# A linear-attention block with a gated feed-forward on one core: a new written order, ten transposes by DMA, constants set elsewhere, and the last unit's feed-forward in parts

## The chip, the core and the metric

The kernel runs on one core of one Trainium2 chip. The time is device microseconds of one execution, and the median over several runs counts. A profiled execution gives its own time and a trace of every instruction and DMA on the engines PE (matmul), DVE (vector), ACT (scalar), POOL (GpSimd) and SP (which only issues DMAs here).

## What is computed

Shapes: batch 4, 8 heads, 768 steps, head size 48, float32. The attention is a recurrence over time with a decay `w` for every key channel; its output, 3072 rows of 384, goes through a feed-forward layer of width 1024 with a softmax-scaled activation, a normalization and a gain.

```python
for t in range(S):
    cur = einsum('bhd,bhe->bhde', u * k[t], v[t])
    y[t] = einsum('bhd,bhde->bhe', r[t], state + cur)
    state = w[t][..., None] * state + einsum('bhd,bhe->bhde', k[t], v[t])
x = y as [B*S, H*D]
h = x @ w_in
solu = h * softmax(h)
ln = (solu - mean) / sqrt(var + 1e-6) * g_ln
out = ln @ w_out
```

## The kernel before, in words

Time is cut into six chunks of 128 steps, and with four batches this makes 24 units; unit `i` is chunk `i // 4` of batch `i % 4`. A unit goes through some thirty stages, each a short function. What stage of which unit runs when is not found by loops: the string ORDER (line 21) lists all of it, about 900 words, and the last loop (line 522) calls one function for each. A word is a stage, the unit's number and, after a dot, the engine (`a` ACT, `d` DVE, `p` POOL), the issuing queue (`s` SP, `a` ACT) or the PSUM bank (`s0` to `s3` one bank, `b0` and `b1` two banks). `InOrder` (line 75) keeps each engine's instructions in the written order; an engine waits where its next instruction's operands are not there. So what stands between two words on one engine is what that engine does in between.

The stages, by their words:
- Loads: LW, LK, LR, LV fetch w, k, r, v of a unit, 192 KB each, in pieces of 192 bytes, into rings of NIO = 7 buffers. LI0 to LI2 (512 KB each) fetch w_in, LO0 and LO1 (768 KB each) w_out, LG and LU the gain and u.
- Attention: lw is the logarithm of the decays (ACT), cum sums them over time (PE), ex takes the exponential (ACT), kp scales k and r with it (DVE), krk and krr transpose the scaled k and r by PE (four each), kr copies them to SBUF. M makes the scores (PE), m copies them and masks them (on DVE, or on ACT with the mask sel on POOL). p, q, dg, dv make the term with u (POOL and DVE); vb rounds v. S, et, st carry the state to the next chunk. Y makes the attention output (PE), y copies it to SBUF.
- Feed-forward: X transposes y by PE (three), xT copies it, H makes h for all 1024 columns (24 matmuls of 128 columns), e is its exponential (ACT), he their product (DVE), hq its square. Oa and Ob multiply by w_out, four of eight column blocks each; for each block there is a matmul of 385 columns (384 outputs and the sum) and two of one column (softmax sum and square sum), all into one PSUM bank. sq, qm, lv (two ACT instructions: lv and rs) make the scale, o applies it, out stores 192 KB from SP.
- Once: wi rounds w_in to bf16; gw multiplies w_out by the gain, mn and mc take its column mean, ce subtracts it; Oa of unit 0 needs all of these. us and uc spread u over the partitions. hot only keeps PE busy.

The constants (masks, identity, block patterns) are set by DVE and POOL ahead of the first word. Two stages are defined and not called: `turned_kr` (line 444), which transposes a unit's scaled k and r from SBUF to SBUF by one DMA on SP, and `turned_x` (line 447), which does so for y.

Of the kernel before, what the change touches and what calls it, by code (L numbers as in the profile page):

```python
# [8 lines left out]
F32 = mybir.dt.float32  # L9
BF16 = mybir.dt.bfloat16  # L10
# [11 lines left out]
LW0.a LK0.s LU0.a LR0.s LW1.a LW2.s hot4.s3 LG0.s LK1.s lw0 LV0.a cum0.b0 LR1.s us0.s0 ex0 hot2.s3 uc0 lw1 LV1.s  # L22
p0 kp0 LW3.a LK2.a LR2.s krk0.s3 q0 krr0 cum1.b1 kr0.a hot2.s2 LV2.s LK3.a M0.b0 LR3.s p1 gs0.s1 ex1 m0.d
hot3.s3 LI1.s lw2 q1 dg0 cum2.b0 lw3 hot2.s3 kp1 vb0.p LI0.a S0.s2 dv0 vb1.a dg1 hot1.s3 ex2 Y0.is0 et0 LV3.a
cum3.b1 LI2.s p2 kp2 krk1.s3 gc0 LO0.s ex3 st0 LW4.s krk2.s1 q2 krr1 LO1.s krr2 kp3 kr1.a hot3.s2 dv1 LK4.s
kr2.d y0.a p3 M1.b0 LK5.a S1.s2 dg2 krk3.s3 vb2.a m1.d krr3 et1 wi0.a S2.s0 wi1.p M2.b1 st1 X0.s1 kr3.a m2.d
Y1.is2 LR4.s wi2.p et2 y1.a M3.b0 xT0.d LV4.a X1.s3 q3 m3.d H0.b1 dv2 gw1.a dg3 gw2.d e0 Y2.is2 LW5.s xT1.d
gw3.p st2 H1.b0 y2.a he0 lw4 gw0.a X2.s1 LR5.s e1 gw7.d cum4.b1 gw4.d hot2.s3 gw6.d gw5.d ex4 he1 vb3.p mn0.s3
LW6.s LV5.a dv3 xT2.a LK6.s kp4 S3.s0 mc0 Y3.is2 LR6.s lw5 ce6.d krk4.s1 ce3.d hq0.a cum5.b0 ce4.d krr4 ce2.d
H2.b1 ce7.d ex5 LW7.s ce1.d ce5.d ce0.d y3.a LK7.s p4 kp5 et3 Oa0.s3 lw6 e2 LR7.s kr4.d p5 krk5.s2 cum6.b0 st3  # L30
hq1.a Ob0 vb4.p he2 LW8.s q4 krr5 ex6 S4.s1 LK8.s kr5.d sq0 M4.b1 lw7 Oa1.s0 kp6 et4 m4.a LR8.s X3.s2 qm0 st4
vb5.p M5.b0 xT3.a cum7.b1 dg4 sel4 lv0 krk6.s1 LV6.s Ob1 m5.d ex7 LW9.s dv4 lw8 S5.s2 kp7 o0.a krr6 LK9.s p6
cum8.b0 sq1 et5 Y4.ns3 kr6.d ex8 H3.b1 q5 LV7.s y4.d hq2.a kp8 q6 LR9.s krk7.s1 e3 X4.s3 st5 LW10.s vb6.p M6.b0
krr7 xT4.d Oa2.s2 dg5 m6.a LK10.s qm1 kr7.d dv5 krk8.s3 lv1 Ob2 he3 out0 sel6 o1.a lw9 M7.b0 out1 dg6 S6.s1 sq2
m7.a LV8.s hq3.d krr8 cum9.b1 LR10.s Y5.ns0 vb7.p qm2 kr8.d lv2 H4.b0 p7 LW11.s et6 y5.d ex9 st6 p8 lw10 kp9
LV9.s X5.s3 S7.s0 e4 Oa3.s1 q7 o2.d vb8.a he4 out2 cum10.b1 dv6 xT5.a krk9.s2 et7 LK11.s ex10 Y6.ns3 q8 krr9 st7
LV10.s H5.b0 hq4.a kp10 sel7 LR11.s kr9.a y6.d M8.b1 dg7 LW12.s S8.s0 lw11 m8.d Ob3 dv7 et8 e5 LV11.s vb9.p
krk10.s3 st8 X6.s2 LK12.s p9 M9.b1 he5 xT6.a Y7.ns0 sq3 m9.a krr10 LR12.s S9.s2 dg8 cum11.b0 et9 LW13.s y7.d
H6.b1 lw12 dv8 ex11 kr10.d LK13.s p10 qm3 lv3 kp11 Oa4.s0 LR13.s e6 q9 st9 X7.s3 cum12.b0 LW14.s xT7.a Ob4 he6
p11 ex12 LV12.s krk11.s2 sel9 sq4 Y8.ns3 o3.a kp12 H7.b1 hq5.a out3 vb10.p qm4 y8.d q10 LK14.s lv4 dg9 M10.b0 e7  # L40
Oa5.s1 LR14.s m10.d vb11.p q11 o4.a krr11 LW15.s X8.s3 lw13 dg10 Ob5 p12 xT8.a out4 he7 kr11.a S10.s0 dv9 S11.s3
LV13.s dg11 sq5 hq6.a Y9.ns2 vb12.p qm5 cum13.b0 y9.d dv10 LK15.s H8.b1 et10 ex13 st10 LR15.s et11 lw14 kp13
Oa6.s2 LW16.s e8 hq7.d krk12.s0 lw15 M11.b0 p13 st11 LK16.s Ob6 lv5 he8 o5.a q12 krr12 m11.a Y10.ns3 out5 kr12.d
krk13.s1 cum14.b1 LR16.s y10.d sq6 krr13 sel11 ex14 cum15.b0 LW17.s kr13.d Oa7.s0 ex15 qm6 LV14.s kp14 p14
Y11.ns3 lw16 X9.s1 Ob7 kp15 lv6 dv11 LK17.s vb13.a xT9.d p15 o6.a M12.b1 y11.d M13.b0 m12.a X10.s1 out6 m13.d
krk14.s2 q13 S12.s3 LR17.s hq8.a krr14 H9.b1 dg12 LV15.s vb14.p xT10.d sq7 q14 et12 qm7 st12 LW18.s lv7 krk15.s1
dg13 e9 X11.s3 sel12 H10.b0 o7.d kr14.a out7 he9 dv12 LK18.s Y12.ns0 xT11.a p16 krr15 LR18.s Oa8.s2 e10 y12.d
kr15.d q15 LV16.s cum16.b1 he10 S13.s0 ex16 dv13 Ob8 LV17.s et13 kp16 q16 X12.s3 LW19.s Y13.ns1 sq8 xT12.a st13
M14.b0 vb15.p M15.b1 LK19.s m14.a y13.d krk16.s3 S14.s0 hq9.d krr16 LR19.s m15.a S15.s1 p17 qm8 kr16.d H11.b0
LW20.s et14 dg14 lv8 sel14 st14 et15 LK20.s dg15 H12.b1 e11 vb16.p o8.d sel15 st15 out8 lw17 Oa9.s3 he11 LV18.s  # L50
e12 vb17.p dv14 S16.s0 LV19.s hq10.a he12 Ob9 dv15 LR20.s et16 cum17.b0 st16 q17 Y14.ns2 LV20.s ex17 X13.s1
y14.d M16.b1 sq9 Oa10.s0 lw18 kp17 LW21.s m16.a Y15.ns2 qm9 xT13.d LK21.s cum18.b0 hq11.d lv9 krk17.s1 lw19
H13.b1 LR21.s o9.d p18 vb18.a dg16 ex18 LV21.s y15.d dv16 krr17 e13 Ob10 kp18 LW22.s sel16 X14.s3 hq12.a kr17.d
S17.s2 LK22.s cum19.b0 q18 he13 Oa11.s1 xT14.a LR22.s ex19 p19 X15.s3 lw20 M17.b1 out9 xT15.d Ob11 sq10 kp19
vb20.p m17.a LW23.s q19 Y16.ns3 qm10 dg17 et17 vb19.a cum20.b0 p20 LV22.s y16.d lv10 H14.b1 dg18 sq11 ex20 sel17
LK23.s st17 lw21 o10.d LR23.s Oa12.s3 e14 kp20 dv17 krk18.s2 Ob12 out10 hq13.a p21 qm11 he14 krk19.s0 LV23.s
lv11 krr18 q20 cum21.b0 sq12 o11.d krr19 ex21 H15.b1 p22 qm12 kr18.d out11 lv12 kr19.d vb21.p Oa13.s1 dv18 kp21
e15 X16.s2 o12.d Y17.ns0 xT16.a M18.b0 hq14.a y17.d out12 krk20.s3 Ob13 he15 lw22 X17.s0 m18.a krk21.s2 xT17.d
krr20 cum22.b1 dg19 krr21 sq13 sel18 ex22 qm13 S18.s0 dg20 H16.b0 kr20.d hq15.a q21 kr21.d lv13 kp22 Oa14.s3
dv19 e16 dv20 M19.b1 et18 Y18.ns2 he16 m19.a Ob14 lw23 sel19 y18.d M20.b1 sq14 M21.b0 o13.d Oa15.s2 m21.a st18  # L60
out13 m20.d krk22.s1 X18.s0 cum23.b0 xT18.a krr22 Ob15 ex23 hq16.d vb22.p dg21 kr22.a Y19.ns0 q22 kp23 H17.b1
vb23.a dv21 qm14 sq15 y19.d lv14 Y20.ns1 e17 p23 o14.d H18.b0 dg22 out14 sel21 qm15 y20.d lv15 krk23.s0 he17 e18
Oa16.s3 dv22 krr23 o15.a he18 q23 Ob16 kr23.a out15 X19.s1 M22.b1 xT19.d M23.b0 hq17.d X20.s2 S19.s0 xT20.a
hq18.d Oa17.s1 m22.a dg23 Y21.ns2 et19 m23.a sel22 st19 H19.b1 sq16 sel23 qm16 y21.d lv16 Oa18.s0 e19 dv23
X21.s2 Ob17 he19 H20.b0 sq17 o16.d xT21.d out16 Y22.ns3 qm17 e20 Y23.ns2 y22.d Ob18 y23.d hq19.a he20 H21.b1
lv17 o17.d X22.s3 Oa19.s2 e21 out17 xT22.d hq20.d X23.s1 sq18 H22.b0 he21 xT23.d Ob19 qm18 hq21.d e22 H23.b1
sq19 lv18 qm19 he22 Oa20.s3 e23 o18.d hq22.d Oa21.s1 out18 lv19 he23 Ob20 o19.d Ob21 sq20 hq23.d out19 Oa22.s0
sq21 qm20 qm21 lv20 Oa23.s2 lv21 o20.d o21.d out20 Ob22 out21 Ob23 sq22 qm22 lv22 sq23 qm23 o22.d lv23 out22
o23.a out23
# [27 lines left out]
def kernel(  # L97
# [14 lines left out]
    C = 128  # L112
# [20 lines left out]
    def bank(shape, dtype, slot, name):  # L133
# [15 lines left out]
    dve.memset(warm, 0.0)  # L149
    uti_neg = consts.tile([C, C], BF16)  # L150
    pool.memset(uti_neg, -1.0)
    pool.affine_select(out=uti_neg, in_=uti_neg, compare_op=ALU.is_ge, fill=0.0, base=0,
                       pattern=[[1, C]], channel_multiplier=-1)
    uts = consts.tile([C, C], BF16)
    pool.memset(uts, 1.0)
    pool.affine_select(out=uts, in_=uts, compare_op=ALU.is_gt, fill=0.0, base=0,
                       pattern=[[1, C]], channel_multiplier=-1)
    ident_f = consts.tile([C, C], F32)
    pool.memset(ident_f, 0.0)
    pool.affine_select(out=ident_f, in_=ident_f, compare_op=ALU.not_equal, fill=1.0, base=0,  # L160
                       pattern=[[-1, C]], channel_multiplier=1)
    ident = consts.tile([C, C], BF16)
    pool.tensor_copy(out=ident, in_=ident_f)

    halves = consts.tile([C, C], BF16)
    pool.memset(halves, 0.0)
    pool.memset(halves[0:2, :], 1.0)
    pool.affine_select(out=halves[0:2, :], in_=halves[0:2, :], compare_op=ALU.is_ge, fill=0.0, base=0,
                       pattern=[[1, C]], channel_multiplier=-64)
    pool.affine_select(out=halves[0:2, :], in_=halves[0:2, :], compare_op=ALU.is_gt, fill=0.0, base=64,  # L170
                       pattern=[[-1, C]], channel_multiplier=64)
    off_blocks = consts.tile([C, HP, 2], BF16)
    pool.memset(off_blocks, 0.0)
    pool.memset(off_blocks[0:2], -30000.0)
    pool.affine_select(out=off_blocks[0:2], in_=off_blocks[0:2], compare_op=ALU.not_equal, fill=0.0, base=0,
                       pattern=[[0, HP], [-1, 2]], channel_multiplier=1)

    one_col = consts.tile([C, 2], BF16)
    dve.memset(one_col, 1.0)
    inv_col = consts.tile([C, 1], BF16)  # L180
    dve.memset(inv_col, 1.0 / RDF)
    ones_row = consts.tile([1, C], F32)
    dve.memset(ones_row, 1.0)

    lw_t = ring("lw", NLW, [C, H, 64], BF16)
    kp_t = ring("kp", NKP, [C, 2, H, 64], BF16)
# [369 lines left out]
```

The softmax here doesn't subtract the row's maximum and nothing guards it: scores larger than these inputs give would overflow.

## Time and profile before

| | |
|---|---|
| Median of 3 runs | 152.28 us (151.85 to 153.1) |
| Profiled execution, its own time | 153.27 us |
| Its span, first to last instruction | 151.6 us |
| Busy: PE, weight load | 137.2 us (91%), 106.6 us (70%) |
| Busy: DVE, ACT, POOL | 127.9 us (84%), 117.9 us (78%), 94.9 us (63%) |
| Moved by DMA | 27.08 MB, 179 GB/s on the mean |

Busy time is the sum over the whole span, and the span has stages that are limited by different things. Two more views are needed: the page's 40 slices of 3.8 us, in which a digit is the busy share in tenths, and the chain of waits, which follows the end back to what released it. Nearly all instructions carry line 89, that of the recorder, so groups are told apart by the tile that they write: `o_ps` is Oa and Ob, `h_ps` is H, `kr_ps` is krk and krr, `x_ps` is X. Matmuls overlap in the pipeline: the mean of one (325 ns for o_ps, 219 ns for h_ps) is longer than its share of PE's time.

### The profile page before, as it was taken

The numbers are of one execution on the slowest core, as the hardware profiler recorded it, in microseconds if no ns is written. First come the engines' busy times: TensorE is split into PE (matmuls) and PEld (weight loads), VectorE is DVE, ScalarE is ACT, GpSimd is POOL, SyncE is SP. The second block draws the span as 40 slices with busy tenths as digits, with TensorE's granted clock in tenths as the row PEclk, the third lists the DMA queues.
The fourth block names the chain that finished last, engine by engine and source line by source line (L and its number), as shares of the span: only waits on it lengthen the run. The fifth ranks groups of instructions, "written<-read, shape, count | busy, mean of one in ns | idle before, by whom it ended". The sixth has DMA issues, their size and how long they took to land.

```text
span 151.6 us, 5258 instructions
## 1 busy us (share of the span) xinstructions
PE 137.2 (91%) x2156; PEld 106.6 (70%) x2158; DVE 127.9 (84%) x235; ACT 117.9 (78%) x238; POOL 94.9 (63%) x127
## 2 busy tenths in 40 slices
PE   4799787879999997999988999999999999999980
PEld 1145566467788776888777797878887888889650
DVE  5209797999999996999976999999998998688940
ACT  3465766599999997999798688999898997484442
POOL 7484993531879859993849999299847682500000
PEclk9999999999999999999999999999999999999997
DMA  5999999999983999989699999898950111011142
GB/s 110 259 257 334 405 335 255 178 210 188 224 179 121 229 217 193 215 176 241 142 243 208 230 175 232 162 230 193 248 164 6 52 56 52 4 52 56 52 160 104
DMA packets 104825, 27.08 MB, mean 179 GB/s; under 512 B 100313, under 2 KB 104418, under 8 KB 104802
## 3 DMA queue, kind: packets, MB, share of 16 engines
q1 hardware_dynamic: 94256, 24.26, 69.6%
q10 hardware_dynamic: 10546, 2.49, 7.3%
q8 instruction: 17, 0.28, 0.7%
q14 instruction: 6, 0.05, 0.1%
HBM read 22.03 MB, written 4.72 MB: 176 GB/s over the span
## 4 chain that ended last, share of the span: by engine, by line
PE 54%; DMA 12%; SPq 10%; DVE 8%; ACT 6%; POOL 4%; issue 4%; ACTq 0%; POOLq 0%
PE o_ps L89 22%; PE h_ps L89 13%; SPq L89 10%; DMA w_in<-in_w_dram 6%; PE kr_ps L89 4%; PE y_ps L89 4%; DMA kr_in<-in_r_dram 4%; PE s_ps L89 3%; PE cum_ps L89 3%; PE m_ps L89 3%; DMA v_in<-in_v_dram 3%; PE x_ps L89 2%; DVE he L89 1%; POOL m L89 1%; DVE w L89 1%
## 5 line engine op out<-in xcount | busy, mean ns | idle before, releaser
L89 PE MATMUL o_ps<-w,he 128*128 128x385 bf16 x192 | 45.7, 325 | 0.1
L89 PE MATMUL h_ps<-xT,win_sb 128*128 128x128 bf16 x576 | 35.9, 219 | 0.3 <-DVE xT L89 0.3
L89 PEld LDWEIGHTS <-win_sb 128*128 128x128 bf16 x576 | 33.0, 98 | 0.9 <-issue 0.4
L89 PE MATMUL o_ps<-inv_col,e 128*128 128x1 bf16 x192 | 31.7, 165 | 0.0
L89 DVE TENSOR_TENSOR he<-h_ps,e 128x1024 bf16<-128x1024 f32 x24 | 29.1, 1216 | 2.7 <-ACT e L89 2.5
L89 PE MATMUL o_ps<-one_col,hq 128*128 128x1 bf16 x192 | 31.3, 163 | 0.0
L89 ACT ACTIVATE e<-h_ps 128x1024 bf16<-128x1024 f32 x24 | 24.5, 1020 | 4.7 <-PE h_ps L89 4.6
L89 DVE TENSOR_TENSOR kp<-cum_ps,kr_in 128x768 bf16<-128x768 f32 x24 | 22.7, 948 | 5.9 <-ACT cum_ps L89 5.6
L89 PEld LDWEIGHTS <-hq 128*128 128x128 bf16 x192 | 18.5, 96 | 12.8
L89 POOL TENSOR_TENSOR p<-kr_in 128x384 bf16<-128x384 f32 x24 | 24.4, 1018 | 3.7 <-DMA kr_in<-in_r_dram 3.6
L89 POOL TENSOR_TENSOR dv<-vb,dg 128x384 bf16<-128x384 bf16 x24 | 19.8, 830 | 9.6 <-DVE dg L89 7.4
L89 POOL TENSOR_SCALAR_AFFINE_SELECT m<-m 128x1024 bf16<-128x1024 bf16 x15 | 16.8, 1120 | 13.4 <-ACT sq L89 5.8
L89 POOL TENSOR_TENSOR q<-p,u_bc 128x384 bf16<-128x384 bf16 x24 | 21.8, 911 | 1.9 <-ACT u_bc L89 1.7
L89 PEld LDWEIGHTS <-kp 128*128 128x128 bf16 x272 | 17.4, 98 | 6.0 <-DVE kp L89 2.1
L89 ACT ACTIVATE cum_ps<-cum_ps 128x768 f32<-128x768 f32 x24 | 19.2, 802 | 3.0 <-PE cum_ps L89 2.9
L89 PE MATMUL kr_ps<-ident,kp 128*128 128x128 bf16 x192 | 18.0, 222 | 2.3 <-ACT gr L89 0.8
L89 PEld LDWEIGHTS <-he 128*128 128x128 bf16 x192 | 18.4, 96 | 0.9
L89 PEld LDWEIGHTS <-e 128*128 128x128 bf16 x192 | 18.4, 96 | 0.5 <-issue 0.2
L89 ACT ACTIVATE lw<-w_in 128x384 bf16<-128x384 f32 x24 | 12.4, 523 | 4.1 <-DMA w_in<-in_w_dram 4.1
L89 ACT CAST m<-m_ps 128x1024 bf16<-128x1024 f32 x15 | 15.0, 1013 | 0.7 <-PE m_ps L89 0.6
L89 DVE TENSOR_TENSOR m<-m_ps,keep 128x1024 bf16<-128x1024 f32 x9 | 10.9, 1215 | 4.2 <-PE m_ps L89 4.2
L89 ACT ACTIVATE hq<-he 128x1024 bf16<-128x1024 bf16 x13 | 13.7, 1057 | 0.0
(82 smaller groups left out, 262.5 us busy)
## 6 DMA issues: line engine op xcount, KB each, us to landing
kr_in<-in_r_dram SPq DMA_DIRECT2D x24, 192.0 KB, 4.3
out_dram<-o SPq DMA_DIRECT2D x24, 192.0 KB, 3.2
kr_in<-in_k_dram SPq DMA_DIRECT2D x21, 192.0 KB, 3.5
w_in<-in_w_dram SPq DMA_DIRECT2D x21, 192.0 KB, 4.2
v_in<-in_v_dram SPq DMA_DIRECT2D x20, 192.0 KB, 4.1
wout_f<-in_moe_w_out_dram SPq DMA_DIRECT2D x2, 768.0 KB, 7.7
win_f<-in_moe_w_in_dram SPq DMA_DIRECT2D x2, 512.0 KB, 5.1
v_in<-in_v_dram ACTq DMA_DIRECT2D x4, 192.0 KB, 4.2
```

Source lines behind the costliest of these rows:

```text
L89: made = make(*args, **kwargs)
```

## The change

- ORDER is written anew. The first loads come in another order and on other queues: LW0 to LW2 and R0, R1 ahead of K0, and all of units 0 to 4 and W5 stand ahead of the second half of w_out. Engines of some copies change.
- For units 19 to 23 krk, krr, kr and X, xT are gone; KD and XD, the two stages on SP that were not called, take their place.
- The constants move into a stage `pc`: the memsets to DVE, four selects stay on POOL; `halves` and `off_blocks` use partitions 0 and 32 and need no select; `keep` and `uts` are one tile. u and the row of ones are bf16 for the u matmul.
- Fifteen stores and LG are issued from POOL.
- Unit 23: H is made in two halves (Ha, Hb), e, he, hq likewise; the three sums go to a PSUM bank of their own (Sa, Sb), the left and right 192 output columns to a bank each (Mal, Mbl and Mar, Mbr), with two scalings and two stores.

```diff
 ORDER = """
-LW0.a LK0.s LU0.a LR0.s LW1.a LW2.s hot4.s3 LG0.s LK1.s lw0 LV0.a cum0.b0 LR1.s us0.s0 ex0 hot2.s3 uc0 lw1 LV1.s
-p0 kp0 LW3.a LK2.a LR2.s krk0.s3 q0 krr0 cum1.b1 kr0.a hot2.s2 LV2.s LK3.a M0.b0 LR3.s p1 gs0.s1 ex1 m0.d
-hot3.s3 LI1.s lw2 q1 dg0 cum2.b0 lw3 hot2.s3 kp1 vb0.p LI0.a S0.s2 dv0 vb1.a dg1 hot1.s3 ex2 Y0.is0 et0 LV3.a
-cum3.b1 LI2.s p2 kp2 krk1.s3 gc0 LO0.s ex3 st0 LW4.s krk2.s1 q2 krr1 LO1.s krr2 kp3 kr1.a hot3.s2 dv1 LK4.s
-kr2.d y0.a p3 M1.b0 LK5.a S1.s2 dg2 krk3.s3 vb2.a m1.d krr3 et1 wi0.a S2.s0 wi1.p M2.b1 st1 X0.s1 kr3.a m2.d
...
-hq18.d Oa17.s1 m22.a dg23 Y21.ns2 et19 m23.a sel22 st19 H19.b1 sq16 sel23 qm16 y21.d lv16 Oa18.s0 e19 dv23
-X21.s2 Ob17 he19 H20.b0 sq17 o16.d xT21.d out16 Y22.ns3 qm17 e20 Y23.ns2 y22.d Ob18 y23.d hq19.a he20 H21.b1
-lv17 o17.d X22.s3 Oa19.s2 e21 out17 xT22.d hq20.d X23.s1 sq18 H22.b0 he21 xT23.d Ob19 qm18 hq21.d e22 H23.b1
-sq19 lv18 qm19 he22 Oa20.s3 e23 o18.d hq22.d Oa21.s1 out18 lv19 he23 Ob20 o19.d Ob21 sq20 hq23.d out19 Oa22.s0
-sq21 qm20 qm21 lv20 Oa23.s2 lv21 o20.d o21.d out20 Ob22 out21 Ob23 sq22 qm22 lv22 sq23 qm23 o22.d lv23 out22
-o23.a out23
+LG0.p pc0 LW0.s LR0.a LU0.s LW1.a hot6.s3 LW2.a LR1.s lw0 ur0 LK2.s LK0.a cum0.b0 LW3.s us0.s0 LK1.a hot4.s3 ex0
+LR2.s LV0.a lw1 lw2 LK3.s cum1.b1 uc0 hot4.s3 kp0 p0 ex1 LW4.a kp1 krk0.s3 q0 gs0.s2 LR3.a cum2.b0 krr0 ex2
+hot2.s1 vb0.p kr0.d LV1.s p1 S0.s1 LK4.a dg0 krk1.s0 LR4.s lw3 M0.b1 hot5.s3 q1 m0.d LI0.s dv0 lw4 dg1 cum3.b1
+et0 p2 hot3.s3 kp2 LV2.a ex3 cum4.b0 q2 LI1.a krr1 kp3 krk2.s3 ex4 LO0.s p3 krr2 kr1.d gc0 vb1.a LW5.s krk3.s2
+st0 LI2.a krr3 dg2 p4 LV4.s M1.b1 LV3.a S1.s0 kp4 kr2.a hot3.s1 m1.d wi0.p LO1.s et1 kr3.a M2.b0 krk4.s1 LK5.s
...
+xT14.d H13.b0 o9.d ex19 out9 lw21 kp19 krk18.s2 e13 Oa11.s3 dg17 KD19 hq12.d krr18 xT15.a H14.b1 lv10 he13
+kr18.a LK22.s LR22.s Y16.ns0 o10.d e14 cum20.b0 LW23.s y16.d S16.s2 dg18 vb17.a Oa12.s1 out10 et16 he14 hq13.a
+dv17 X16.s0 Ob11 sel17 ex20 st16 cum21.b1 xT16.d sq11 Ob12 kp20 p20 ex21 S17.s2 hq14.a KD20 kp21 vb18.p M18.b0
+q19 Y17.ns0 lw22 qm11 m18.d H15.b1 et17 q20 sq12 KD21 lv11 o11.a qm12 y17.d p21 lv12 M19.b0 st17 LK23.s S18.s3
+lw23 m19.d p22 Oa13.s0 LR23.s e15 out11 dv18 X17.s2 et18 dg19 LV21.s o12.a M20.b0 he15 Ob13 xT17.a q21 m20.a
+Y18.ns1 vb19.p st18 out12 cum22.b1 H16.b0 dg20 ex22 p23 y18.d sq13 qm13 kp22 lv13 Oa14.s2 vb20.p e16 dv19 o13.d
+KD22 M21.b1 q22 X18.s3 m21.a S19.s1 he16 Ob14 vb21.p LV22.s hq15.a out13.p dg21 LV23.s cum23.b1 dg22 H17.b0 dv20
+et19 sq14 ex23 qm14 dv21 xT18.a kp23 Y19.ns0 hq16.a sel20 Oa15.s3 st19 KD23 lv14 y19.d H18.b1 q23 o14.a vb22.a
+XD19 sel21 e17 Oa16.s1 dv22 e18 Ob15 he17 out14.p Y20.ns0 he18 Ob16 hq17.a M22.b0 sq15 y20.d M23.b1 Y21.ns2
+m22.d m23.a XD20 Oa17.s0 hq18.a y21.d sel23 H19.b1 dg23 XD21 sq16 vb23.a qm15 lv15 dv23 Y22.ns2 e19 H20.b0 y22.d
+o15.d XD22 qm16 he19 Oa18.s2 out15.p e20 Ob17 he20 H21.b1 sq17 lv16 hq19.d qm17 o16.d Y23.ns3 lv17 Ob18 hq20.a
+y23.d out16 o17.d XD23 Oa19.s1 sq18 e21 qm18 out17.p Oa20.s3 lv18 H22.b0 o18.d he21 out18.p Ob19 e22 hq21.d
+Ha23.b1 sq19 qm19 he22 lv19 Oa21.s0 ea23 Ob20 hea23 Ob21 sq20 o19.a qm20 hq22.d hqa23.a Hb23 out19.p lv20
+Oa22.s2 sq21 eb23 qm21 o20.a heb23 Sa23.s1 lv21 Ob22 out20.p hqb23.d o21.d Sb23 sq22 Mal23.s3 qm22 out21.p sq23
+lv22 Mar23.s0 qm23 Mbl23 lv23 o22.d Mbr23 ol23.a out22.p or23.d outl23 outr23.a
 """
...
-    pool.memset(uti_neg, -1.0)
-    pool.affine_select(out=uti_neg, in_=uti_neg, compare_op=ALU.is_ge, fill=0.0, base=0,
-                       pattern=[[1, C]], channel_multiplier=-1)
...
-    pool.tensor_copy(out=ident, in_=ident_f)
...
+    ident_f = consts.tile([KF, KF], F32)
+    ones_row = consts.tile([1, C], BF16)
+    keep = uts
+
+    def constants(i, x):
+        dve.memset(warm, 0.0)
+        dve.memset(uti_neg, -1.0)
+        dve.memset(uts, 1.0)
+        dve.memset(ident, 0.0)
+        dve.memset(ident_f, 0.0)
+        pool.affine_select(out=uti_neg, in_=uti_neg, compare_op=ALU.is_ge, fill=0.0, base=0,
+                           pattern=[[1, C]], channel_multiplier=-1)
+        pool.affine_select(out=uts, in_=uts, compare_op=ALU.is_gt, fill=0.0, base=0,
+                           pattern=[[1, C]], channel_multiplier=-1)
+        pool.affine_select(out=ident, in_=ident, compare_op=ALU.not_equal, fill=1.0, base=0,
+                           pattern=[[-1, C]], channel_multiplier=1)
+        pool.affine_select(out=ident_f, in_=ident_f, compare_op=ALU.not_equal, fill=1.0, base=0,
+                           pattern=[[-1, KF]], channel_multiplier=1)
+        dve.memset(one_col, 1.0)
+        dve.memset(inv_col, 1.0 / RDF)
+        dve.memset(ones_row, 1.0)
+
+        dve.memset(halves, 0.0)
+        dve.memset(off_blocks, 0.0)
+        for row, own in ((0, 0), (32, 1)):
+            dve.memset(halves[row:row + 1, 64 * own:64 * own + 64], 1.0)
+            dve.memset(off_blocks[row:row + 1, :, 1 - own], -30000.0)
+        for j in range(max(NLW, NKP)):
+            if j < NLW:
+                dve.memset(lw_t[j][:, :, D:], 0.0)
+            if j < NKP:
+                dve.memset(kp_t[j][:, :, :, D:], 0.0)
+        dve.memset(mean_w, -1.0 / DF)
+        dve.memset(w2[:, :, DM:], 1.0 / RDF)
...
+    u_b = consts.tile([1, DM], BF16)
...
-    queue = {"s": sp, "a": act}
+    queue = {"s": sp, "a": act, "p": pool}
...
+    def round_u(i, x):
+        dve.tensor_copy(out=u_b, in_=u_row)
...
-        pe.matmul(ps["u"], lhsT=ones_row, rhs=u_row, start=True, stop=True)
+        pe.matmul(ps["u"], lhsT=ones_row, rhs=u_b, start=True, stop=True)
...
-    def hidden(i, x):
-        xT = xT_t[i % NWK]
-        h_ps = live[i]["h_ps"] = bank([128, KF, C], F32, x, "h_ps")
-        for f in range(KF):
+    def hidden_part(i, f0, f1):
+        xT, h_ps = xT_t[i % NWK], live[i]["h_ps"]
+        for f in range(f0, f1):
             for j in range(KM):
                 pe.matmul(h_ps[:, f, :], lhsT=win_sb[:, j, f * 128:(f + 1) * 128], rhs=xT[:, j, :],
                           start=(j == 0), stop=(j == KM - 1))
 
-    def hidden_exp(i, x):
-        act.activation(out=e_t[i % NWK], in_=live[i]["h_ps"], func=EXP)
-
-    def hidden_mul(i, x):
-        dve.tensor_mul(out=he_t[i % NWK], in0=live[i]["h_ps"], in1=e_t[i % NWK])
-
-    def hidden_square(i, x):
-        he, hq = he_t[i % NWK], hq_t[i % NWK]
+    def hidden(i, x):
+        live[i]["h_ps"] = bank([128, KF, C], F32, x, "h_ps")
+        hidden_part(i, 0, KF)
+
+    def hidden_a(i, x):
+        live[i]["h_ps"] = bank([128, KF, C], F32, x, "h_ps")
+        hidden_part(i, 0, KF // 2)
+
+    def hidden_b(i, x):
+        hidden_part(i, KF // 2, KF)
+
+    ALL, LOW, HIGH = slice(0, KF), slice(0, KF // 2), slice(KF // 2, KF)
+
+    def hidden_exp(i, x, part=ALL):
+        act.activation(out=e_t[i % NWK][:, part], in_=live[i]["h_ps"][:, part], func=EXP)
+
+    def hidden_mul(i, x, part=ALL):
+        dve.tensor_mul(out=he_t[i % NWK][:, part], in0=live[i]["h_ps"][:, part], in1=e_t[i % NWK][:, part])
+
+    def hidden_square(i, x, part=ALL):
+        he, hq = he_t[i % NWK][:, part], hq_t[i % NWK][:, part]
         if x == "a":
             act.activation(out=hq, in_=he, func=SQUARE)
         else:
...
                       skip_group_check=True)
 
     def output_a(i, x):
-        live[i]["o_ps"] = bank([C, DM + 3], F32, x, "o_ps")
+        L = live[i]
+        L["o_ps"] = bank([C, DM + 3], F32, x, "o_ps")
+        L["o"], L["sums"] = L["o_ps"][:, :DM], L["o_ps"][:, DM:]
         output(i, 0)
 
     def output_b(i, x):
         output(i, 1)
 
+
+    HALF = {"l": slice(0, DM // 2), "r": slice(DM // 2, DM)}
+
+    def columns_of(i, x, side, part):
+        if part == 0:
+            live[i]["o" + side] = bank([C, DM // 2], F32, x, "o_ps")
+        for f in range(part * KF // 2, (part + 1) * KF // 2):
+            pe.matmul(live[i]["o" + side], lhsT=he_t[i % NWK][:, f, :], rhs=w2[:, f, HALF[side]],
+                      start=(f == 0), stop=(f == KF - 1))
+
+    def sums_of(i, x, part):
+        if part == 0:
+            live[i]["sums"] = bank([C, 3], F32, x, "o_ps")
+        to = live[i]["sums"]
+        for f in range(part * KF // 2, (part + 1) * KF // 2):
+            pe.matmul(to[:, 0:1], lhsT=he_t[i % NWK][:, f, :], rhs=w2[:, f, DM:], start=(f == 0), stop=False,
+                      skip_group_check=True)
+            pe.matmul(to[:, 1:2], lhsT=e_t[i % NWK][:, f, :], rhs=inv_col, start=False, stop=False,
+                      skip_group_check=True)
+            pe.matmul(to[:, 2:3], lhsT=hq_t[i % NWK][:, f, :], rhs=one_col[:, :1], start=False, stop=(f == KF - 1),
+                      skip_group_check=True)
+
     def sums(i, x):
-        act.activation(out=sq_t[i % NWK], in_=live[i]["o_ps"][:, DM:DM + 2], func=SQUARE)
+        act.activation(out=sq_t[i % NWK], in_=live[i]["sums"][:, 0:2], func=SQUARE)
 
...
-    def scaled_out(i, x):
-        o_ps, rs, o = live[i]["o_ps"], rs_t[i % NWK], o_t[i % NWK]
+    def scaled_out(i, x, side=""):
+        rs, o = rs_t[i % NWK], o_t[i % NWK][:, HALF.get(side, slice(0, DM))]
         if x == "d":
-            dve.tensor_scalar(out=o, in0=o_ps[:, :DM], scalar1=rs, scalar2=None, op0=MULT)
+            dve.tensor_scalar(out=o, in0=live[i]["o" + side], scalar1=rs, scalar2=None, op0=MULT)
         else:
-            act.activation(out=o, in_=o_ps[:, :DM], func=COPY, scale=rs)
-
-    def store(i, x):
+            act.activation(out=o, in_=live[i]["o" + side], func=COPY, scale=rs)
+
+    def store(i, x, side=""):
         c, b = units[i]
-        sp.dma_start(out=out[b * S + c * C:b * S + (c + 1) * C, :], in_=o_t[i % NWK])
+        cols = HALF.get(side, slice(0, DM))
+        queue[x or "s"].dma_start(out=out[b * S + c * C:b * S + (c + 1) * C, cols], in_=o_t[i % NWK][:, cols])
+
+    def of_part(stage, *part):
+        return lambda i, x: stage(i, x, *part)
 
     stages = dict(
+        pc=constants,
...
+        Ha=hidden_a, Hb=hidden_b,
+        **{name + tag: of_part(stage, part) for name, stage in dict(e=hidden_exp, he=hidden_mul, hq=hidden_square).items()
+           for tag, part in (("a", LOW), ("b", HIGH))},
+        **{name + side: of_part(stage, side) for name, stage in dict(o=scaled_out, out=store).items() for side in "lr"},
+        **{name + tag + side: of_part(columns_of, side, part) for name in "M" for tag, part in (("a", 0), ("b", 1))
+           for side in "lr"},
+        Sa=of_part(sums_of, 0), Sb=of_part(sums_of, 1),
```

## The prediction

> **What bounds the kernel now.** I read the page's slices first, then its chain of waits, then busy time by stretches, then the landings of the early loads, then the waits.
>
> ```profile
> PE   4799787879999997999988999999999999999980
> DMA  5999999999983999989699999898950111011142
> 34.00:146.40 112.40, 109.94 (x1882) 90.41 (x1880) 103.83 (x176) 95.21 (x196) 73.16 (x86) 1.00 0.71 156
> 92.00:146.00 54.00, 53.94 (x915) 44.43 (x914) 49.78 (x88) 42.97 (x90) 27.91 (x33) 1.00 0.45 109
> ```
>
> A slice is 3.8 us. DMA is full from the second slice to the 29th (110 us) and nearly empty after; PE has gaps in the first nine slices and none that shows after. In the stretch rows the columns are the length, then PE, weight load, DVE, ACT and POOL busy, clock, DMA share, GB/s. So there are three stages: loads set the pace up to about 34 us, PE from there to 146.4 us (DVE close behind with 103.8 of 112.4), and a tail that is pure latency. In the second stage a microsecond taken from PE's own work is worth a microsecond, if nothing new is waited for. What a stage costs PE stands in the chain, as one piece for one stage:
>
> ```profile
> 105.84 0.47 PE kr_ps L89 x8
> 121.96 1.34 PE h_ps L89 x24
> 129.49 0.83 PE o_ps L89 x12
> 135.65 0.17 PE x_ps L89 x3
> 140.38 5.98 PE o_ps L89 x84
> 146.38 0.18 ACT sq L89
> 148.20 0.58 ACT o L89
> ```
>
> Columns: start, length, engine and tile, instructions. I use such spacings and not the page's durations, since matmuls overlap (219 ns each, but 24 of them in 1.34 us): krk with krr 0.46, X 0.18, H 1.34, Oa or Ob 0.83, M 0.33, S 0.47, Y 0.38, cum 0.33. All words of the order summed this way, without warm-ups, make 123 us of PE. At 33.73 us, where the first Oa starts, 108.0 of it is left; PE ends at 146.36, so this stage holds 146.36 - 33.73 - 108.0 = 4.6 us of scattered waits. The start is read from these waits:
>
> ```profile
> POOL vb L89 <- DMA v_in<-in_v_dram: 6.1, 4, 2.8
> ACT lw L89 <- DMA w_in<-in_w_dram: 4.1, 3, 2.2
> POOL p L89 <- DMA kr_in<-in_r_dram: 3.6, 3, 2.0
> DVE w L89 <- ACT mean_sb L89: 0.4, 1, 0.4
> ```
>
> (Total us, times, longest.) From the completion events in the trace: a 192 KB load lands every 0.83 us early on, the weights (3 MB) come at about 400 GB/s, LI2 lands at 18.54, LO1 at 24.96; from there gains, column mean and centring on DVE take until 33.67, and Oa0 starts.
>
> [...] loads of both queues land interleaved at one rate. [...] in this trace TensorE does eight in 0.47 us, since they are pipelined; no DMA transpose occurs in it. [...] no DMA is issued from POOL before.
>
> **The change part by part.**
>
> **Transposes of units 19 to 23.** Removed from PE: 5 x 0.46 (k, r) + 5 x 0.18 (y) = 3.2 us, all in the PE-bound stage: whole gain. Gone too are ten PSUM copies (0.35 to 1.02 us each) on DVE and ACT; with the reassignments DVE falls by 6 us in sum and ACT rises by 2.5. Nothing on those is booked: PE hides them. Added: ten DMA transposes on SP, where loads 22 and 23 and four stores stand behind them. What covers them is PE work between producer and consumer: from KD19, 20, 21, 22, 23 to the M of that unit 8.3, 3.9, 5.9, 8.9 and 4.6 us; from Y19 to Y23 to the H of that unit 7.3, 4.8, 6.0, 7.6 and 5.1, of which some 1.2 us go to the y copy and its turn on DVE. A small DMA out of SBUF here takes 1.82 us at the least from issue to landing (the stores near 132 us). [...] I take 4 and 3 us: about 1 us of wait in all, at M20 and H20. No gain beyond the 3.2 is possible from it.
>
> **The start.** Before LO1's landing 17 unit loads have to land in the old order, 21 in the new (five full units and W5), and two of the three w_in parts wait on ACT's queue behind its compute. Four more loads x 0.83 = 3.3 us: LO1 at 28.2. By the same count LI2 comes at about 24 instead of 18.5. K0 is issued behind lw0 on ACT, so kp0 (6.55 before) comes at about 9; PE is idle then, so I book nothing. From LO1 on, ACT does gw0, gw3, gw6, xT3, ex5, e2, mc0 and DVE he2 and seven centrings; with the rows' durations Oa0 starts at 37.3 against 33.73. But PE has by then done more: 18.9 us of useful work precede Oa0 in the new order, against 15.1. What is left is 101.3. So the later start and the larger share done before cancel, within 1.5 us either way, and what stays is the 3 us less PE work: 37.3 + 101.3 + 4.6 = 143.2 for PE's end, against 146.4. I keep the 4.6 us of scattered waits: DVE is lighter, but new waits on POOL stand against it.
>
> **Constants and u.** POOL's row of constants ran from 0.80 to 4.83; now DVE does the memsets (about 1 us more before kp0, which waits for DMA anyway), and POOL four selects of 0.29 us after the issue of LG. cum0 started at 4.89, waiting for lw0 until W0 had landed at 4.29: cover of 2 us. u in bf16 shortens the u matmul from 1.64 us at a time when PE idles. Ten more warm-up matmuls (0.21 each) fill the same idle time. All zero; without that cover at most 1 us.
>
> **Stores on POOL.** Fifteen stores leave SP. [...] POOL has 73 us of work in 112, so it has room, but it is in order: out7 waits for o7 ahead of dv and vb work. Zero, to +1.5.
>
> **The tail.** Before, after PE's end at 146.36: sq, qm, lv, rs for two units, o, issue at 148.80, landing at 150.65, end at 151.6: 5.2 us. After, the sums of unit 23 are complete before its 16 column matmuls (about 0.08 each, 1.3 us by half of 0.165), which covers the 0.9 us of sq, qm, lv, rs. After PE's end there remain half an o (about 0.4), issue and landing 1.85, and the end 0.95: 3.3 to 3.5. Gain 1.7. PE pays 0.25 for the extra columns, which the 101.3 holds already. The halves of e and he let PE wait less for H23, where Ob20 and Oa21 cover it anyway.
>
> **Sum.** -3.2 (PE's end) - 1.7 (tail) + 1.0 (transposes) = -3.9: span 147.7 against 151.6. The profiled execution itself took 153.27, 1.0 over the median of 152.28 shown; carried to the median, 148.4.
>
> **The rivals.** (1) *Slower: the DMA transposes outlast their cover.* Place: M20 and M21, H20 and Ha23, where PE is in order and everything behind waits. Price: with 8 us for k, r and 6 for y, about 3 + 2 at the two M and 2.4 + 0.5 + 1.5 at the H, some 9 us: 152.28 - 4.9 + 9 = 156. [...] It decides from where waits exceed 4.9 us: about 6 us for k, r and 5 for y. For it: KD20, KD21 are issued back to back behind three loads at one queue; 128-row transposes by DMA are nowhere in the trace. Against: DMA is nearly idle after 110 us, and the stores land in 1.8. (2) *The start costs what the rest brings.* If the weights behind ACT's compute come 3 us later than counted, Oa0 is at 40.5 and the gain shrinks to 0.9: 151.4. For it: ACT waited 2.5 us for a DMA slot ahead of gw before. [...] (3) *Larger gain*: lighter DVE removes 2 us of scattered waits, no transposing wait: 145.4. (4) *The change doesn't do what it says*, the transposes serializing with all loads: that is (1).
>
> **How the numbers follow.** A measurement here tells 1% (1.5 us: 150.8 to 153.8) from no change. Forecast 0.52 (146.5 to 150.5), larger gain 0.12, start 0.13 (half of it still within 1%, little beyond), slower 0.23. Faster 0.64, same 0.13, slower 0.23. Range: 144.8 leaves out under a tenth below, 155.0 about an eighth above. The likeliest case's own range is 146.5 to 150.5.
>
> **What would show it.** In the new trace: Oa0 near 37 us; LO1 landing near 28; PE busy to about 143; no kr_ps and x_ps for the last units and the transposes landing in 3 to 4 us; last store issued about 1 us after PE's end. Wrong: PE waits at M or H of units 20 to 23 on DMA of more than 1 us each; Oa0 after 39; DVE or POOL waits of over 6 us in the middle.

## The result, and the profile after

The change made the kernel slower.

| | before | after |
|---|---|---|
| Median on one chip | 152.69 us (151.85 to 153.33, 4 runs) | 156.98 us (156.39 to 158.15, 4 runs) |
| Ratio, 95% interval | | 1.0294 [1.0204, 1.0384] |
| Profiled execution, own time | 153.27 us | 157.55 us |
| Its span | 151.6 us | 155.5 us |
| First Oa starts | 33.73 us | 43.45 us |
| Last matmul ends (modelled) | 147.20 us | 151.46 us |

The runs of one kernel here lie 0.3 to 4.4% apart, and a ratio is made without the runs that lie over 1.5% above the fastest of their kernel, so it can differ from the quotient of two medians.

The slices of the page of after (3.9 us each; PE, granted clock and DMA):

```profile
PE   6889768749789999999999997899999999999990
PEclk9999999999968999999999999999999999999997
DMA  5999999899989982499985999996999792254023
```

PE has its gaps up to the twelfth slice, three further than before, and again in the 25th and 26th (93 to 101 us); the clock digits "68" lie right behind the first matmuls of Oa. DMA is now busy after 110 us too: with the transposes, and with loads that go out later than before (V23 at 123.82 us, against 108.27). The chain of waits (start, length, what) shows what set the start:

```profile
24.20 3.79 SPq L88
28.04 3.76 DMA kr_in<-in_r_dram
31.82 0.41 ACTq L88
32.24 0.05 issue
32.28 1.03 ACT e L88
33.34 1.22 DVE he L88
...
38.77 1.10 issue
39.88 1.89 DVE w L88 x3
41.77 1.01 issue
42.78 0.62 DVE w L88 x2
43.45 1.04 PE o_ps L88 x12
```

The odd step is the second and third. The load of r of unit 6 lands at 31.80 us; only then does ACT issue its load of v of unit 5; and only then does ACT compute `e` of unit 0, whose H (24 matmuls from 28.73 us, 1.34 us of PE) had been there since about 30.1. ACT's own timeline (start, length, queue or engine, operation, and in brackets the idle time before) shows the like further up:

```profile
15.22 0.46 ACTq L88 DMA_DIRECT2D kr_in<-in_k_dram  x1
15.73 0.94 ACT L88 ACTIVATE lw<-w_in 128x384 bf16<-128x384 f32 x2 [2.34 <-DMA win_f<-in_moe_w_in_dram]
...
16.94 2.55 ACTq L88 DMA_DIRECT2D win_f<-in_moe_w_in_dram  x1
...
20.49 0.35 ACTq L88 DMA_DIRECT2D win_f<-in_moe_w_in_dram  x1
...
27.63 1.04 ACT L88 CAST win_sb<-win_f 128x1024 bf16<-128x1024 f32 x1 [1.58 <-DMA win_f<-in_moe_w_in_dram]
...
31.82 0.41 ACTq L88 DMA_DIRECT2D v_in<-in_v_dram  x1
32.28 1.02 ACT L88 ACTIVATE e<-h_ps 128x1024 bf16<-128x1024 f32 x1 [2.85 <-PE y_ps L88]
```

The bracket of the last line blames y_ps. The completion events of this trace tell more. The landings of SP's and ACT's DMAs are told there by eight semaphores. For 99 issues the landing of the DMA before on the same semaphore can be read: none of the 99 goes out ahead of it, and eight of ACT's follow it within 0.03 us. K4 (15.22) follows the landing of R4 at 15.20, LI2 (20.49) that of V4 at 20.47, V5 (31.82) that of R6 at 31.80. LI1 (16.94), issued while DMA was full, took 2.55 us on ACT's queue. ACT's computing stood idle for 2.85 us, until V5 was out. And LI2 went out at 20.49 and landed at 27.61, while LO1, on SP, overtook it and landed at 23.39.

### The profile page after: what moved, and what is told of

It is laid out like the page before. It is cut to its first block, busy times and chain, and to the rows that moved or that the text cites. A ratio compares the mean times of both kernels' runs of the same rounds, so it can differ in the third digit from the quotient of the medians.

```text
span 155.5 us, 5239 instructions
## 1 busy us (share of the span) xinstructions
PE 137.7 (89%) x2127; PEld 105.5 (68%) x2127; DVE 125.0 (80%) x232; ACT 118.8 (76%) x244; POOL 101.5 (65%) x131
## 4 chain that ended last, share of the span: by engine, by line
PE 46%; DMA 12%; issue 11%; SPq 10%; DVE 7%; ACT 6%; POOL 3%; POOLq 0%; ACTq 0%; DVEq 0%
PE o_ps L88 16%; PE h_ps L88 11%; SPq L88 10%; DMA kr_in<-in_r_dram 5%; DMA wout_f<-in_moe_w_out_dram 4%; PE kr_ps L88 4%; PE s_ps L88 4%; DMA kr<-kp 3%; PE y_ps L88 3%; PE cum_ps L88 3%; PE m_ps L88 3%; DVE he L88 2%; DVE w L88 2%; POOL out_dram L88 2%; ACT e L88 2%
## 5 line engine op out<-in xcount | busy, mean ns | idle before, releaser
L88 PE MATMUL o_ps<-w,he 128*128 128x385 bf16 (+2 forms) x208 | 46.5, 317 | 2.5 <-DVE w L88 1.8
L88 DVE TENSOR_TENSOR he<-h_ps,e 128x1024 bf16<-128x1024 f32 (+1 forms) x25 | 29.3, 1176 | 4.8 <-ACT e L88 4.6
L88 ACT ACTIVATE e<-h_ps 128x1024 bf16<-128x1024 f32 (+1 forms) x25 | 24.6, 986 | 5.5 <-PE y_ps L88 2.8
L88 PEld LDWEIGHTS <-he 128*128 128x128 bf16 x208 | 19.6, 96 | 0.6
L88 POOL TENSOR_SCALAR_AFFINE_SELECT m<-m 128x1024 bf16<-128x1024 bf16 x13 | 14.2, 1089 | 8.1 <-ACT m L88 8.1
L88 PEld LDWEIGHTS <-kp 128*128 128x128 bf16 x232 | 15.0, 99 | 5.8 <-issue 3.2
L88 POOL DMA_DIRECT2D out_dram<-o x15 | 8.5, 569 | 15.8 <-ACT o L88 6.2
L88 ACT ACTIVATE hq<-he 128x1024 bf16<-128x1024 bf16 (+1 forms) x17 | 17.5, 1031 | 0.4 <-DVE he L88 0.4
L88 PE MATMUL kr_ps<-ident,kp 128*128 128x128 bf16 x152 | 14.9, 226 | 2.0 <-ACT gr L88 1.9
L88 ACT CAST m<-m_ps 128x1024 bf16<-128x1024 f32 x13 | 13.2, 1012 | 3.5 <-PE m_ps L88 3.3
```

What stands on the lines that cost most here:

```text
L88: made = make(*args, **kwargs)
```

## The experiments

**One load.** V5 of the changed kernel from SP in place of ACT.

```diff
-LV5.a
+LV5.s
```

> The changed kernel with one load (v of unit 5) issued from SP instead of ACT, at the same place of the order. Theory 1, the loss arises in the start, where loads on ACT's queue wait for the landing of an earlier DMA and hold the computations behind them: the first exponential of the feed-forward (e of unit 0), at 32.28 us after a wait of 2.85, starts at about 30.1, the first Oa at 41 to 42 instead of 43.45, and the time falls by 1.5 to 2.5 us to 154.5 to 155.5. Theory 2, the DMA transposes of units 19 to 23 cost the time: e of unit 0 may move, the time stays at 156 to 158. Theory 3, the stores on POOL: no change.

154.13 us, 1.0101 [1.002, 1.0183]. In ACT's timeline:

```profile
30.36 1.02 ACT L86 ACTIVATE e<-h_ps 128x1024 bf16<-128x1024 f32 x1 [0.73 <-PE h_ps L86]
```

One letter brings `e` of unit 0 1.9 us forward, the first Oa from 43.45 to 41.88 us, and the time from 1.029 to 1.010 of before. The profiled span falls by 3.2 us, twice what the first Oa gains: in this run PE's clock stays full (1.0 on the mean, against 0.982), where after had 3.4 us at half clock behind Oa.

**Six loads.** All late loads of ACT from SP.

```diff
-LK4.a LV2.a LI1.a LI2.a LV3.a LV5.a
+LK4.s LV2.s LI1.s LI2.s LV3.s LV5.s
```

> The changed kernel with six loads that stand on ACT's queue ahead of or among its computations (k of unit 4, v of 2, 3 and 5, second and third part of w_in) issued from SP, same places in the order. Theory 1 (start, ACT held by its loads): ACT no longer waits for DMA slots, the third part of w_in lands at 24 to 25.5 us instead of 27.6, the first Oa starts at 38 to 40 instead of 43.45, PE's clock does not fall there, and the time is 151 to 153.5. Theory 2 (transposes) or 3 (POOL stores): within 1 us of 157.

152.54 us, 0.9975 [0.9925, 1.0025]: the whole loss is gone. LI2 lands at 22.82 in place of 27.61, LO1 at 27.34, and

```profile
27.23 1.02 ACT L86 ACTIVATE e<-h_ps 128x1024 bf16<-128x1024 f32 x1 [0.48 <-PE h_ps L86]
```

The first Oa is at 39.42. LI2 and LO1 are now within 1.2 us of the prediction's count, so the count of bytes holds where no load waits on ACT.

**POOL beside the centring.** The centring on DVE was slow as well. DVE's and POOL's timelines of after:

```profile
39.88 3.79 DVE L88 TENSOR_TENSOR w<-w,mean_sb 128x384 bf16<-128x384 bf16 x7
```

```profile
40.55 1.02 POOL L88 TENSOR_TENSOR q<-p,u_bc 128x384 bf16<-128x384 bf16 x1
41.54 1.11 POOL L88 TENSOR_TENSOR p<-kr_in 128x384 bf16<-128x384 f32 x1
```

The single additions behind the x7 take 347 ns alone, and 1065 and 1146 ns beside POOL's q and p. In this run the six loads are on SP, and POOL waits for a centred block before it goes on:

```diff
+    def hold_pool(f, x):
+        pool.tensor_copy(out=scrap, in_=w2[:, f, :1])
...
-ce3.d
+ce3.d ho3
```

> The changed kernel with the six loads on SP (as in a_loads_sp) and, in addition, POOL made to wait: one tiny copy on POOL that reads a column written by the last centring on DVE stands ahead of vb of unit 6, q of 5 and p of 6, so that POOL does nothing while DVE centres w_out. Theory 1 with this addition ([...] 1065 and 1146 ns beside POOL, 347 ns alone): all seven adds take about 350 ns, the first Oa starts at 37.3 to 37.8 instead of 39.42, and the time falls by 1 to 2 us from 152.5, to 150.5 to 151.5. If the long adds have another cause: they stay, Oa at 39.4, 152.5 or above.

153.04 us, 0.9984 [0.9944, 1.0024].

```profile
35.70 1.96 DVE L86 TENSOR_TENSOR w<-w,mean_sb 128x384 bf16<-128x384 bf16 x7
```

The centring falls from 3.79 to 1.96 us and the first Oa to 37.45 us, and the end doesn't move. That POOL's work beside it slowed the centring is shown, its worth is nil: from the first Oa to its end PE now takes 109.0 us in place of 106.8 with the six loads alone. In the middle ACT now waits for loads of w, where the kernel with the six loads alone has no such wait and after has one of 2.2 us (total us, times, longest; 45 to 110 us):

```profile
ACT lw L86 <- DMA w_in<-in_w_dram: 3.6, 4, 1.2
```

**Fewer loads.** Do the late loads pace the middle? The last version and the kernel before, each with 13 loads of r left out.

```diff
-LR8.s LR9.s LR10.s
...
-LR19.s LR20.s
```

> The version with six loads on SP and POOL held behind the centring, with the loads of r of units 8 to 20 left out (those units use the r of an earlier unit that is still in the buffer; 2.5 MB less). Theory (late loads pace the middle): ACT's waits for w_in in 45 to 110 us (3.6 us) go, PE waits after the first Oa fall from 7.7 to about 5 us, ratio 0.975 to 0.985 against 0.998 for the version with all loads. Rival (engines pace the middle): ratio 0.993 to 1.000, waits of PE after Oa unchanged within 0.7 us.

> The kernel before with the same 13 loads of r left out (units 8 to 20 use the r of an earlier unit). Both theories: PE is the bound there, ratio 0.990 to 1.000. If it falls as much as the other kernel does, loads pace the middle in both orders, and not in the new one alone.

150.12 us, 0.9756 [0.9604, 0.9908], and 150.86 us, 0.9875 [0.9787, 0.9963], from five runs each. The first gain lies where the theory put it, the second just beyond what was expected of the kernel before, with an interval that reaches into it. From the first Oa to PE's end the first falls from 109.0 to 106.3 us (in a trace of the longest of its five runs), the second from 113.5 to 110.3. The 46 to 110 us of before, then of before with fewer loads (length; PE, weight load, DVE, ACT, POOL busy; clock, DMA share, GB/s):

```profile
46.00:110.00 64.00, 61.54 (x1069) 50.94 (x1062) 59.81 (x101) 57.37 (x118) 52.58 (x63) 1.00 0.96 202
```

```profile
46.00:110.00 64.00, 63.86 (x1117) 53.29 (x1118) 62.53 (x107) 60.04 (x124) 53.43 (x64) 1.00 0.82 178
```

With DMA at 0.82 PE fills the stage, with 0.96 it misses 2.5 us. So loads take their share of the middle in both orders, and not in the new one alone; engines that are ready earlier meet loads that are not. (Leaving loads out can also change which load waits for which; that share wasn't separated.)

**The same loads in the order of before.** It has two such waits: ACT idle 2.48 us ahead of gw0, for V4, and 1.87 us ahead of xT2, for V5.

```diff
-LV3.a LK5.a LV4.a LV5.a
+LV3.s LK5.s LV4.s LV5.s
```

> The kernel before with LV3, LK5, LV4 and LV5 issued by SP in place of ACT. Theory (a load that ACT issues waits for the landing of an earlier DMA and holds ACT's computing): ACT's wait of 2.48 us ahead of gw0 and the 1.87 us ahead of xT2 are gone, Oa of unit 0 starts 1 to 2 us ahead of the 33.7 us, and the time falls by 0 to 1.5 us (ratio 0.990 to 1.000), since a start earlier than the middle can use gave nothing before. Rival (the loads' bandwidth sets the start): Oa of unit 0 within 0.4 us of 33.7, ratio 1.00.

153.88 us, 1.0022 [0.9988, 1.0055]; the first Oa at 34.69, 1 us later. A miss. Those two waits on ACT are gone, but a load that stayed on ACT now waits: LI0 goes out at 14.18 us, 0.02 after R3's landing (12.68 before), and lands at 20.65 in place of 18.54. ACT stands still behind it, in this row under R3's name:

```profile
ACT vb L86 <- DMA kr_in<-in_r_dram: 2.6, 1, 2.6
```

And the eight centring additions, now beside POOL's q and vb, took 3.44 us in place of 2.48. Moving these loads moved more than their waits, and this run does not tell what the order of before would gain with no load waiting on ACT. The same with the last unit in parts:

> The kernel before with those four loads on SP and the last unit's feed-forward in parts. If both gains are real and add: ratio 0.985 to 0.993, end of PE to end of span about 4 us. If the tail gives nothing that can be measured, the same ratio as with the loads alone within 0.3%.

153.34 us, 0.9988 [0.9946, 1.003]: nothing to be told apart.

**Constants.** The change's code for constants and u in the order of before.

```diff
-LW0.a LK0.s
+pc0 LW0.a LK0.s
...
-lw0
+lw0 ur0
```

> The change's code for constants and u, with before's order of everything else (and the last unit whole, stores on SP). The prediction's step says zero: ratio 0.995 to 1.005, first kp within 0.3 us of 6.55 us. Rival (the constants on DVE come late): first kp 1 us later and a ratio up to 1.007.

155.53 us, 1.0129 [1.0071, 1.0188]. The first kp is at 6.48 us, as told, yet 1.3% are lost. The waits have fallen otherwise: V3, which went out in before at 15.45, 0.02 us after LI1's landing, goes out at 13.18, ahead of LO1. V4 in its turn now follows LO1's landing at 25.18, in place of V3's at 23.49:

```profile
25.20 0.40 ACTq L86 DMA_DIRECT2D v_in<-in_v_dram  x1
25.70 0.62 ACT L86 ACTIVATE w<-wout_f,gr 128x384 bf16<-128x384 f32 x1 [3.88 <-DMA wout_f<-in_moe_w_out_dram]
```

`e` of unit 0 starts 1.7 us later and the first Oa 1.4 us later: the same hold on ACT, made by a step that is itself free.

**Transposes alone.** In the order of before: k, r and y; the same again with more rounds; k and r alone; y alone.

```diff
-krk19 krr19 kr19
+KD19
...
-X19 xT19
+XD19
```

> The kernel before with only this part of the change: units 19 to 23 have their k, r and y transposed by DMA on SP, each placed right after its producer, all else in the old order. Theory 1: the transposes are a gain of about 3 us (5 x 0.46 + 5 x 0.18 of PE), less up to 1 us of waits at H of unit 22, so 149.3 to 150.5. Theory 2 (transposes cost the time): 154 or more.

> The same kernel as b_turns, with more rounds, since its profiled span was 0.6 us shorter than before's and its runs were longer. If the transposes by DMA gain what the span shows: 151.5 to 152.5. If the longer runs are its true time: 153.5 to 155.

> The kernel before with only k and r of units 19 to 23 transposed by DMA; y stays on PE. PE loses 5 x 0.46 = 2.3 us of work; the waits of M on these DMAs were 1.1 us in b_turns. If these waits are the whole price: 1.2 us gained, 151.3 to 152. If the price lies elsewhere (DMA queue, clock): no gain, 152.7 or more.

> Only the y transposes of units 19 to 23 by DMA, in the order of before. Prediction's step: 0.9 us of PE work saved, waits at H small where the cover of 5 to 7 us holds, ratio 0.994 to 1.000. Rival (the DMA's latency is given back as waits): ratio 1.000 to 1.008, with PE waiting 0.5 us or more for xT<-y.

1.0136 [1.0024, 1.0248] from two runs, and again, from ten, 1.0018 [0.9981, 1.0055]; k and r alone 1.006 [1.0023, 1.0096]; y alone 0.9983 [0.9948, 1.0018], with PE's end 1.1 us earlier in its profile and no wait of PE for xT. So y may give what was said, though its interval takes in no change as well, and k, r give it back. SP's queue in the second run shows a part of why:

```profile
109.00 2.50 SPq L85 DMA_TRANSPOSE kr<-kp  x1
111.55 0.58 SPq L85 DMA_DIRECT2D out_dram<-o  x1
112.22 0.39 SPq L85 DMA_DIRECT2D v_in<-in_v_dram  x1
112.71 0.64 SPq L85 DMA_DIRECT2D out_dram<-o  x1
113.44 1.33 SPq L85 DMA_TRANSPOSE kr<-kp  x1
```

kp of unit 21 was done at 108.5, its transpose was issued at 113.44 and landed at 117.05, just before M of the unit starts (117.09), after 0.82 us in which PE idled. From 100 us on PE idles 1.9 us more than in before, out of 3.2 us saved; this wait and one of 0.25 us for an xT make up 1.1 of it, and the rest wasn't traced.

**Stores.** The fifteen stores from SP in the changed kernel, and from POOL in the kernel before.

```diff
-out14.p
+out14
```

> The changed kernel with all fifteen stores that it issues from POOL back on SP. Theory 1: POOL is not on the path, within 1 us of 157. Theory 3, POOL held by stores that wait for their o (12 us of such waits on POOL), so that dv and the masks behind come late: 153 to 155.5.

> The kernel before with the same fifteen stores issued by POOL. Theory (stores on POOL cost at the end only): the last store lands about 2.2 us after its issue, the span ends 1.3 us after that landing, the own time lies about 2.1 us above the span in place of 1.7, first Oa and PE's end as before; ratio 1.003 to 1.008. Rival (POOL, in order, is held by stores that wait for o and delays dv and vb): PE's end more than 0.7 us later, ratio 1.006 to 1.015. If it costs nothing: 0.998 to 1.002.

The first scattered from 154.19 to 160.83 us and gave no ratio. In its trace PE's end is as in after (151.55), with the first Oa 1.3 us later (44.74); from there PE took 106.8 us, against 106.4 with V5 from SP and the stores on POOL, so no cost of the stores in the middle shows. The second: 158.31 us, 1.0393 [1.0327, 1.0459], far outside both theories. DVE's group of the squares, first in before, then with the stores on POOL (busy us, mean ns):

```profile
L89 DVE TENSOR_TENSOR hq<-he 128x1024 bf16<-128x1024 bf16 x11 | 8.2, 757 | 0.0
```

```profile
L86 DVE TENSOR_TENSOR hq<-he 128x1024 bf16<-128x1024 bf16 x11 | 14.9, 1363 | 0.0
```

POOL, which works in order, now also stands before stores whose o isn't there yet (total us, times, longest):

```profile
POOL out_dram L86 <- DVE o L86: 18.2, 8, 5.2
```

POOL is held, then, as the rival said, at more than the rival's 1.5%. Each store takes it some 0.6 us besides, so that its work falls elsewhere against DVE's, and the first three squares, which took 0.78, 0.68 and 1.42 us, take 3.11, 1.77 and 3.95 beside it. PE's end is 3.5 us later, and from there to the span's end it takes 5.11 us in place of 4.36. That is 4.2 of the 6 us (that the squares make up PE's share of it is argued from the trace and wasn't tried apart); the profiled execution was the shortest of its six, and the rest isn't seen in it.

**The last unit.** Its feed-forward in parts in the order of before; then with the y transposes too.

```diff
-H23.b1
+Ha23.b1
...
-o23.a out23
+Mbl23 lv23 o22.d Mbr23 ol23.a out22 or23.d outl23 outr23.a
```

> The kernel before with only the last unit's feed-forward in halves and banks (H, e, he, hq in two halves, sums apart, left and right columns with a store each, from SP and ACT). If the part is worth what the tail of the changed kernel shows (4.1 us from PE's last instruction to the end of the span, 5.2 before, PE paying 0.25): a gain of 0.6 to 1.2 us, 151.7 to 152.3. If the pieces cost more than they save (ten more instructions on ACT and DVE while other units' scales run there): 153 or more.

> The kernel before with the last unit's feed-forward in parts and the y transposes of units 19 to 23 by DMA, loads, constants, k and r and stores as before. If both terms are real and add: ratio 0.990 to 0.996, end of PE to end of span about 4 us, no wait of PE for xT<-y over 0.3 us. If they are nothing: 0.998 to 1.002.

0.9975 [0.9941, 1.0008] alone. Both together: 0.992 [0.9877, 0.9962], 1.2 us under the kernel before, and the only version with all its loads whose interval lies below 1. But only seven of its 22 runs enter, since its fastest (150.72 us) sets the limit low; the medians of all runs are 153.41 and 153.83 us. A gain is likely and not established.

## Why the prediction was wrong

The forecast was 148.4 us, 8.6 below the result. Its span of 147.7 was 7.8 too low; the rest lies between span and median, 1.4 us in place of 0.7. Rival 2 came nearest: its ground, "ACT waited 2.5 us for a DMA slot", is the mechanism, though its text has the weights wait behind ACT's compute. It put the first Oa 3 us late, half of what came.

- **"The start" failed.** It set the first Oa at 37.3, and it came at 43.45: 6.1 of the 7.8 us. The step counted bytes in the order of the words and said of ACT's weights only that they "wait on ACT's queue behind its compute". The reverse binds: ACT's compute waits behind its loads. Taking six loads off ACT gives 4.0 us, holding POOL from the centring another 2.0, and Oa is then at 37.45. (The 18.54 us that it names as LI2's landing before is LI0's, the last of the three parts; LI2's was 16.67. As H needs all three, the count stands.)
- **The end of PE was misread.** 146.36 us is where Ob of unit 22 was done; Ob of unit 23 ran on to 147.20 and is in the 108.0 us of work. On that end the scattered waits are 5.5 us and not 4.6, and the stage from the first Oa comes to 107.8 us. With the start as told, in the run that holds POOL (Oa at 37.45), the span is 150.78, still 3.1 too long: 1.2 in that stage, 0.8 in the tail, 0.8 from this misreading, the rest from the start.
- **"4.6 us of scattered waits": about right in size, not a constant.** After took 108.0 us from the first Oa to PE's end, against 107.8 on the same end. But 3.1 us of the waits of before go with a tenth of the bytes, so most of them were loads, and a start that comes earlier meets more of them. In after the number holds partly by luck: its clock was halved from 44.2 to 47.7 us, which costs some 1.7 us, half of that time (an estimate). The stretch 40 to 50 us of after:

```profile
40.00:50.00 10.00, 8.22 (x99) 5.79 (x97) 9.07 (x17) 7.25 (x14) 4.67 (x6) 0.83 0.99 195
```

- **Transposes: landings and waits right in the new order.** The DMA rows of after have them landing in 4.3 and 2.9 us, where 4 and 3 were taken, an estimate of the author's:

```profile
kr<-kp SPq DMA_TRANSPOSE x5, 4.3
xT<-y SPq DMA_TRANSPOSE x5, 2.9
```

PE waited for one of them, 0.6 us at M20, where about 1 us was put on M20 and H20. Rival 1 fell. What they gain there wasn't measured alone. Where SP's queue isn't arranged for it, as in the order of before, the k, r half loses.
- **Constants: wrong as a zero.** Nothing that waits for them is late, but they reshuffle which load waits for which, and cost 1.3% in the order of before. Their share within the new order wasn't measured alone.
- **Stores: inside "zero, to +1.5" here, far outside in the other order.** The range was the author's estimate. In the new order the end shows about 0.8 us: the last store lands 2.24 us after its issue (1.85 before), and the span ends 1.29 us after that (0.91). In the order of before they cost 6 us. So one price does not hold for both orders; that it goes by what else POOL has to do there is argued from the squares, not shown apart.
- **Tail: 1.7 was mis-sized.** The part itself is as told: 3.28 us from the last matmul to the end with the stores on SP, 3.3 to 3.5 predicted. But the 5.2 us of before ran from 146.36; from the end of the last matmul, as after was counted, they are 4.36. That leaves 1.1, and POOL's stores take 0.8 of it.

What stays open: what k and r turned by PE would give within the new order, the constants there, and a sure number for its stores.

## What to carry to other kernels

Keep loads that may have to wait off an engine that computes: in after ACT's `e` waited 2.85 us behind the issue of a DMA that had nothing to do with it, and the profile put the wait down to another name. It pays only if no other load is made to wait instead: six loads gave 4.9 us in the new order, four gave nothing in the order of before. Look for DMA issues that start within 0.05 us of another DMA's landing. Before an earlier start is priced as an earlier end, ask what the next stage waits for; and before a POOL instruction is added, look which two-input DVE operations it pushes POOL's work beside (the squares took 1363 ns in place of 757 here).

## What was not expected of the hardware

- Two-input DVE operations in SBUF took three times as long and more beside POOL: 1146 ns against 347 (128x384, in after), and from 0.68 us at the least in before to 3.95 at the most with the stores on POOL (128x1024), while he, which reads PSUM, stays at 1216 ns on the mean in these two. Not always: the square at 46.48 us of before took 0.78 us beside POOL's vb.
- In after, a gap of 1.78 us on PE (from 41.67 us, by the modelled ends) was followed by 3.41 us at half clock (from 44.24), and yet a gap of 2.15 us at 32.73 in the same trace by none. What makes the difference was not shown.
- A DMA transpose cost SP's queue mostly 1.2 to 1.5 us to issue (2.06 at the longest in after, 2.50 in the queue shown above), against 0.33 for a store in a quiet queue; in after, landing took 3.4 to 5.0 us for 128x1024 bf16 and 2.3 to 4.2 for 128x384.
